# Decode attention on one core: keys transposed inside their load buffers, queries and results moved in single transfers

## The chip, the core and the metric

The kernel runs on one core of a Trainium2 chip. The core has a matrix engine (TensorE, "PE" in the profile; its weight loads are listed as "PEld"), a vector engine (VectorE, "DVE"), a scalar engine (ScalarE, "ACT"), GpSimd ("POOL") and SyncE ("SP"), which here only issues transfers. Sixteen DMA engines move data between the chip's main memory (HBM) and the on-chip memory SBUF; matmul results go to a smaller memory, PSUM. Both on-chip memories have 128 partitions. The metric is the device time of one execution in microseconds (us), and a kernel's time is the median of several runs.

## The reference

One query token attends to 65,536 cached tokens, with 32 query heads and 8 key/value heads, in bfloat16. Four query heads share a key/value head.

```python
B, Hq, Hkv, Sq, Sk, D = 1, 32, 8, 1, 65536, 128
k = jnp.repeat(k, Hq // Hkv, axis=1)
v = jnp.repeat(v, Hq // Hkv, axis=1)
scores = jnp.einsum("bhqd,bhkd->bhqk", q, k) * D ** -0.5
p = jax.nn.softmax(scores, axis=-1)
return jnp.einsum("bhqk,bhkd->bhqd", p, v)
```

Keys and values are 134.2 MB each. Every byte of them is read once and used by four query heads.

## The kernel before

**Loads.** A key/value head's keys are loaded in four steps of 128 partitions x 128 tokens x 128 numbers, 4 MB each (`k_load`, L118 to L122); values likewise (`v_load`, L196). All of these loads are issued by SP, in program order, into four rotating buffers of 32 KB per partition (`iopool`, L56): a load can be issued only when the work on the load four places ahead of it, in the same buffer, has let that buffer go. The order of loads is: four key steps of head 0; then for each head g from 1 to 7 a key step of head g and a value step of head g-1 in turn; at the end four value steps of head 7, the last of which is cut into six pieces.

**Scores.** `k_step(g, s, kn)` (L124) computes the scores of one key step. DVE transposes the keys in 32 x 32 blocks, taking two bfloat16 numbers as one 4-byte element; each transposition (L135) takes two of the eight groups w = 0..7 into a separate tile `T` (three buffers, `tpool`, L57). PE then runs four matmuls for each group (L144), 32 per key step, accumulated in one PSUM bank `sc` (three buffers, L62). ACT copies the finished bank into `S_g` (L151). The weights of these matmuls, `wq`, hold the four queries of the head at a shifted place in a tile of zeros; `queries(g)` (L104) fills them from `qx`, the transposed queries.

**Queries.** At the start ACT's queue issues four transfers of the 32 query rows (256 bytes each) into the four quarters of the partitions of `qn` (L69, L70). DVE transposes `qn` to `qx` (L100) and copies the first head's queries to `wq` (L109) before it starts on the keys.

**Softmax and values.** When a head's four steps of scores are in, `softmax(g)` finds the maximum, ACT takes the exponential over all scores with row sums (L177), and DVE transposes the result to `ET` (L190). `v_stream` (L202 to L213) multiplies each value step with `ET`, 32 matmuls per step, accumulated in `psum_o`; `pick` (L224, L230) reduces that to the head's 128 numbers per query.

**Results.** `finish(g0, n)` sums the partial results of n heads with one matmul, takes the reciprocal of the sums of exponentials (`sums`, L237, L239), and `store` scales (L244) and stores them (L250): heads 0 to 3 at once while head 4's values are next, heads 4 to 6 at once near the end. `finish_last` handles head 7, whose last value step is worked off token by token as its pieces land.

Engines run their own instructions in order. A scheduler places the instructions of all parts on each engine; within the part at stake, PE has the 32 score matmuls of a key step and then the 32 matmuls of the value step that was loaded after it.

Of the kernel before, what the change touches and what calls it, by code (L numbers as in the profile page):

```python
# [8 lines left out]
ALU = mybir.AluOpType  # L9
# [5 lines left out]
NW = 16  # L15
# [5 lines left out]
def kernel(  # L21
# [17 lines left out]
    nc = tc.nc  # L39
    P = nc.NUM_PARTITIONS  # L40
    B, Hq, Sq, D = q.shape
    _, Hkv, Sk, _ = k.shape
    assert B == 1 and Sq == 1 and D == P
    HPG = Hq // Hkv
# [7 lines left out]
    fp32 = mybir.dt.float32  # L52
    bf16 = mybir.dt.bfloat16

    const = ctx.enter_context(tc.tile_pool(name="const", bufs=1))
    iopool = ctx.enter_context(tc.tile_pool(name="iopool", bufs=4))  # L56
    tpool = ctx.enter_context(tc.tile_pool(name="tpool", bufs=3))  # L57
    spool = ctx.enter_context(tc.tile_pool(name="spool", bufs=2))
    epool = ctx.enter_context(tc.tile_pool(name="epool", bufs=2))
    opool = ctx.enter_context(tc.tile_pool(name="opool", bufs=2))  # L60
    stats = ctx.enter_context(tc.tile_pool(name="stats", bufs=2))
    psc = ctx.enter_context(tc.tile_pool(name="psc", bufs=3, space=bass.MemoryType.PSUM))  # L62
    psm = ctx.enter_context(tc.tile_pool(name="psm", bufs=1, space=bass.MemoryType.PSUM))
    psf = ctx.enter_context(tc.tile_pool(name="psf", bufs=1, space=bass.MemoryType.PSUM))
    pso = ctx.enter_context(tc.tile_pool(name="pso", bufs=2, space=bass.MemoryType.PSUM))


    qn = const.tile([P, D], bf16)
    for a in range(4):  # L69
        nc.scalar.dma_start(out=qn[32 * a:32 * a + 32, :], in_=q[0, :, 0, :])  # L70


    WX = P + 32
# [1 line left out]
    for x in range(2):  # L75
# [8 lines left out]
        out=sel[:, :], in_=ident[:, :].rearrange("p (x h) -> p h x", h=HPG), axis=AX.X, op=ALU.max  # L84
# [3 lines left out]
        out=blk[:, :], in_=ident[:, :].rearrange("p (j w h) -> p w j h", w=W, h=HPG), axis=AX.XY, op=ALU.max  # L88
# [6 lines left out]
    nc.gpsimd.memset(one[:, :], 1.0)  # L95
    lsum_all = const.tile([P, Hkv], fp32)
    o_all = const.tile([P, Hkv, D], fp32)

    qx = const.tile([P, D], bf16)
    nc.vector.transpose(out=qx[:, :].bitcast(fp32), in_=qn[:, :].bitcast(fp32))  # L100
# [3 lines left out]
    def queries(g):  # L104
        eng = nc.vector if g == 0 else nc.gpsimd
        wv = Wq[g % 2][:, :].rearrange("p (b r x) -> p b r x", b=2, r=2)
        for a in range(4):
            qd = slice(32 * a, 32 * a + 32)
            eng.tensor_copy(  # L109
                out=wv[qd, :, :, 32 * a + 28:32 * a + 28 + HPG],  # L110
                in_=qv[qd, :, :, g * HPG:(g + 1) * HPG],
            )

    queries(0)

    S_tiles, E_tiles, ET_tiles, o_tiles = {}, {}, {}, {}

    def k_load(g, s):  # L118
        kn = iopool.tile([P, NT, D], bf16, name="kn", tag="io", align_bytes=2048)
        src = k[0, g].rearrange("(p n) d -> p n d", p=P)  # L120
        nc.sync.dma_start(out=kn[:, :, :], in_=src[:, s * NT:(s + 1) * NT, :])
        return kn  # L122

    def k_step(g, s, kn):  # L124
        if s == 0:
            S_tiles[g] = spool.tile([P, KT, 4 * P], fp32, name="S_g")
        wq = Wq[g % 2]
        kv = kn[:, :, :].rearrange("p (c w) d -> p w c d", w=W)
        sc = psc.tile([P, 4 * P], fp32, name="sc")
        for w in range(W):  # L130
            if s == 0 and w == W // 2 and g > 0:
                transpose_weights(g - 1)
            if w % 2 == 0:
                T = tpool.tile([P, 2, NW, D], bf16, name="T")
                nc.vector.transpose(  # L135
                    out=T[:, :, :, :].bitcast(fp32),
                    in_=kv[:, w:w + 2].bitcast(fp32),
                )
            Tv = T[:, w % 2].rearrange("p n (b i r) -> p n b i r", b=2, r=2)
            for b in range(2):  # L140
                for r in range(2):
                    bp = 2 * b + r
                    at = bp * WX + 28 - 4 * w
                    nc.tensor.matmul(  # L144
                        out=sc[:, :],
                        lhsT=wq[:, at:at + P],
                        rhs=Tv[:, :, b, :, r],
                        start=(w == 0 and bp == 0),
                        stop=(w == W - 1 and bp == 3),
                    )  # L150
        nc.scalar.copy(out=S_tiles[g][:, s, :], in_=sc[:, :])  # L151

    def softmax(g):
        S_g = S_tiles[g]
# [32 lines left out]
    def transpose_weights(g):  # L187

        ET = epool.tile([P, KT, NW, 32], bf16, name="ET")
        nc.vector.transpose(  # L190
            out=ET[:, :, :, :].rearrange("p s c x -> p (s c x)"),
            in_=E_tiles[g][:, :, :].rearrange("p s x -> p (s x)"),
        )
        ET_tiles[g] = ET

    def v_load(g, s, pieces=(NT,)):  # L196
        vb = iopool.tile([P, NT, D], bf16, name="vb", tag="io", align_bytes=2048)
        src = v[0, g].rearrange("(p n) d -> p n d", p=P)
        x = 0
        for step in pieces:  # L200
            n0 = s * NT + x
            nc.sync.dma_start(out=vb[:, x:x + step, :], in_=src[:, n0:n0 + step, :])  # L202
            x += step
        return vb

    def v_stream(g, s, vb, rows, last):

        if s == 0:
            o_tiles[g] = pso.tile([P, 4, D], fp32, name="psum_o")
        for c in range(rows // W):  # L210
            for x in range(2):
                j = 2 * x + c % 2
                nc.tensor.matmul(  # L213
                    out=o_tiles[g][32 * j:32 * j + 32, :, :],
                    lhsT=ET_tiles[g][:, s, c, :],
                    rhs=vb[:, c * W + 4 * x:c * W + 4 * x + 4, :],
                    start=(s == 0 and c < 2),
                    stop=(last and c >= rows // W - 2),
                )

    def pick(g):

        o_m = opool.tile([P, 4, D], fp32, name="o_m")
        nc.vector.tensor_tensor(  # L224
            out=o_m[:, :, :],
            in0=o_tiles[g][:, :, :],
            in1=mask[:, :].unsqueeze(2).broadcast_to([P, 4, D]),
            op=ALU.mult,
        )
        nc.vector.tensor_reduce(  # L230
            out=o_all[:, g, :], in_=o_m[:, :, :].rearrange("p x d -> p d x"), axis=AX.X, op=ALU.add
        )

    def sums(g0, n):

        psum_l = psm.tile([HPG, n], fp32, name="psum_l", tag="misc")
        nc.tensor.matmul(out=psum_l[:, :], lhsT=sel[:, :], rhs=lsum_all[:, g0:g0 + n], start=True, stop=True)  # L237
        rl = stats.tile([HPG, n], fp32, name="rl")
        nc.vector.reciprocal(out=rl[:, :], in_=psum_l[:, :])  # L239
        return rl  # L240

    def store(g0, n, psum_f, rl):
        o_out = stats.tile([HPG, n, D], bf16, name="o_out")
        nc.vector.tensor_tensor(  # L244
            out=o_out[:, :, :],
            in0=psum_f[:, :, :],
            in1=rl[:, :].unsqueeze(2).broadcast_to([HPG, n, D]),
            op=ALU.mult,
        )
        nc.scalar.dma_start(  # L250
            out=out[0, :, 0, :].rearrange("(g h) d -> h g d", h=HPG)[:, g0:g0 + n, :], in_=o_out[:, :, :]
        )

    def finish(g0, n):
        rl = sums(g0, n)
        psum_f = psf.tile([HPG, n, D], fp32, name="psum_f", tag="fin")
        nc.tensor.matmul(  # L257
            out=psum_f[:, :, :], lhsT=sel[:, :], rhs=o_all[:, g0:g0 + n, :], start=True, stop=True
        )
        store(g0, n, psum_f, rl)  # L260

    def finish_last(g, s, vb):

# [43 lines left out]
    for g in range(Hkv + 1):  # L307
        if 0 < g < Hkv:
            queries(g)
        for s in range(KT):  # L310
            if g < Hkv:
                k_step(g, s, k_load(g, s))
            elif s == 0:
                transpose_weights(g - 1)
            if g > 0:
                last = s == KT - 1
                if g == Hkv and last:
                    finish_last(g - 1, s, v_load(g - 1, s, pieces=(64, 32, 16, 8, 4, 4)))
                else:
                    v_stream(g - 1, s, v_load(g - 1, s), NT, last)  # L320
                    if last:
                        pick(g - 1)
                    if last and g % 4 == 0:
                        finish(g - 4, 4)
                    if last and g == Hkv - 1:
                        finish(g - g % 4, g % 4)
        if g < Hkv:
            softmax(g)

# [29 lines left out]
```

## Time and profile before

| | |
|---|---|
| Median of 3 runs | 631.85 us (631.57 to 631.90) |
| Profiled execution, its time | 631.69 us |
| Profiled execution, its span (first to last instruction) | 629.6 us |
| PE busy | 363.2 us (58%) |
| DVE busy | 340.4 us (54%) |
| ACT busy | 36.8 us (6%) |
| POOL busy | 6.4 us (1%) |
| HBM read | 268.47 MB, 426 GB/s over the span |
| Mean granted clock of TensorE | 0.780 |

The page also cuts the span into 40 equal slices of 15.74 us and gives, for each, the busy share of each engine in tenths, the granted clock of PE, the mean busy share of the 16 DMA engines and the data rate. A group line names the line of the kernel, the engine, the operation, the tile written and the tiles read with their shapes, then the count, the total busy time in us and the mean of one in ns, and after a second bar the idle time of that engine before these instructions and what ended most of it. In a timeline, the first two columns are the start and the length in us, and an entry may merge several instructions of one line ("x16"). A DMA queue line gives packets, megabytes and the share of the time of the 16 DMA engines.

### The profile page before, as it was taken

Reading aid. Unit: us, or ns where it says so; the run is one execution under the profiler, and the core shown is the slowest. Engines: PE = TensorE matmul, PEld = TensorE weight load, DVE = VectorE, ACT = ScalarE, POOL = GpSimd, SP = SyncE. Lnnn points to the kernel's source line nnn. Section 1 sums busy time; section 2 is a strip of 40 time slices with the busy share of each in tenths; the row PEclk is TensorE's granted clock in tenths of the full one; section 3 lists DMA queues with packets and bytes.
Section 4 is the critical chain, followed back from the end, with each engine's and each line's share of the span. In section 5 each row is a group of like instructions: output and inputs, shape, how many; then the busy total and the mean of one; then the engine's idle time right before and its main releaser. Section 6 shows DMA issues by size and latency. Waiting matters only on the chain.

```text
span 629.6 us, 4872 instructions
## 1 busy us (share of the span) xinstructions
PE 363.2 (58%) x2133; PEld 141.5 (22%) x2133; DVE 340.4 (54%) x201; ACT 36.8 (6%) x49; POOL 6.4 (1%) x37
## 2 busy tenths in 40 slices
PE   0686836745557554575645856447665466644645
PEld 0232312211222221222211222112221122211212
DVE  0998833774337753377543775436754366553511
ACT  0000100010000100001000010001000010000100
POOL 0000000000000000000000000000000000000000
PEclk9998988767887677876778867788677787767856
DMA  8999999999999999999999999999999999999996
GB/s 369 433 434 431 433 432 434 432 433 433 432 433 432 433 433 432 433 432 433 432 433 433 430 434 434 433 432 433 435 432 433 432 433 433 432 433 434 431 430 267
DMA packets 10192, 268.78 MB, mean 427 GB/s; under 512 B 1340, under 2 KB 1596, under 8 KB 1852
## 3 DMA queue, kind: packets, MB, share of 16 engines
q1 hardware_dynamic: 9936, 268.44, 99.0%
q8 instruction: 16, 0.26, 0.1%
q10 hardware_dynamic: 236, 0.04, 0.0%
q14 instruction: 4, 0.03, 0.0%
HBM read 268.47 MB, written 0.01 MB: 426 GB/s over the span
## 4 chain that ended last, share of the span: by engine, by line
DMA 73%; DVE 12%; issue 11%; PE 2%; ACTq 0%; DVEq 0%; SPq 0%
DMA kn<-in_k_dram 66%; DVE T L135 12%; DMA vb<-in_v_dram 5%; DMA qn<-in_q_dram 2%; PE sc L144 2%; PE psum_o L213 0%; PE psum_oT L290 0%; ACTq L70 0%; PE psum_f L280 0%; DVEq L135 0%; DVE wq L109 0%; PE psum_f L287 0%; DVE sel L83 0%; DVE o_last L302 0%; SPq L202 0%
## 5 line engine op out<-in xcount | busy, mean ns | idle before, releaser
L144 PE MATMUL sc<-T,wq 128*128 128x512 bf16 x1024 | 287.9, 445 | 220.2 <-DVE T L135 220.2
L135 DVE STREAM_TRANSPOSE T<-kn 128x2048 f32<-128x2048 f32 x128 | 284.2, 2277 | 198.6 <-DMA kn<-in_k_dram 198.6
L144 PEld LDWEIGHTS <-wq 128*128 128x128 bf16 x1024 | 109.5, 109 | 394.6 <-issue 159.5
L213 PE MATMUL psum_o<-vb,ET 128*32 128x512 bf16 x1008 | 65.1, 403 | 12.0 <-DMA vb<-in_v_dram 9.8
L151 ACT COPY S_g<-sc 128x512 f32<-128x512 f32 x32 | 18.8, 587 | 510.8 <-PE sc L144 510.8
L213 PEld LDWEIGHTS <-ET 128*32 128x32 bf16 x1008 | 25.5, 100 | 49.2 <-issue 28.3
L156 DVE TENSOR_REDUCE mx<-S_g 128x1 f32<-128x2048 f32 x8 | 18.3, 2286 | 26.1 <-ACT S_g L151 26.1
L190 DVE STREAM_TRANSPOSE ET<-E_g 128x2048 bf16<-128x2048 bf16 x8 | 18.5, 2311 | 16.3 <-ACT E_g L177 16.3
L177 ACT ACTIVATE E_g<-S_g,nmb 128x2048 bf16<-128x2048 f32 x8 | 16.0, 2001 | 47.6 <-DVE nmb L174 40.4
L224 DVE TENSOR_TENSOR o_m<-psum_o,mask 128x512 f32<-128x512 f32 x8 | 5.5, 682 | 21.5 <-PE psum_o L213 21.5
L109 POOL COPY wq<-qx 32x16 bf16<-32x16 bf16 x28 | 5.3, 190 | 426.9 <-PE sc L144 410.2
L160 PE MATMUL psum_t<-ident,mx 128*1 128x128 f32 x8 | 2.2, 270 | 11.2 <-DVE mx L156 11.2
L100 DVE STREAM_TRANSPOSE qx<-qn 128x64 f32<-128x64 f32 x1 | 0.2, 245 | 15.0 <-DMA qn<-in_q_dram 15.0
L172 PE MATMUL psum_b<-one,mrow 1*128 1x1 f32 x16 | 3.5, 288 | 8.3 <-DVE mrow L166 8.3
L230 DVE TENSOR_REDUCE o_all<-o_m 128x128 f32<-128x512 f32 x8 | 8.0, 1000 | 0.0
L172 PEld LDWEIGHTS psum_b<-one,mrow 1*128 1x128 f32 x16 | 3.0, 232 | 12.2 <-issue 11.4
L237 PE MATMUL psum_l<-lsum_all,sel 128*4 128x4 f32 (+2 forms) x6 | 0.6, 166 | 7.7 <-ACT E_g L177 7.7
L257 PE MATMUL psum_f<-o_all,sel 128*4 128x512 f32 (+1 forms) x4 | 2.6, 730 | 2.9 <-DVE o_all L230 2.9
L160 PEld LDWEIGHTS psum_t<-ident,mx 128*1 128x1 f32 x8 | 0.6, 79 | 15.1 <-DVE mx L156 11.6
L174 DVE COPY nmb<-psum_b 128x1 f32<-128x1 f32 x8 | 1.2, 152 | 2.9 <-PE psum_b L172 2.9
L290 PE MATMUL psum_oT<-ET,vb 128*128 128x4 bf16 x56 | 1.8, 167 | 1.4 <-DMA vb<-in_v_dram 1.4
L244 DVE TENSOR_TENSOR o_out<-psum_f,rl 4x512 bf16<-4x512 f32 (+1 forms) x2 | 1.2, 612 | 2.5 <-PE psum_f L257 2.5
(30 smaller groups left out, 16.1 us busy)
## 6 DMA issues: line engine op xcount, KB each, us to landing
kn<-in_k_dram SPq DMA_DIRECT2D x32, 4096.0 KB, 29.6
vb<-in_v_dram SPq DMA_DIRECT2D x31, 4096.0 KB, 34.1
vb<-in_v_dram SPq DMA_DIRECT2D x1, 2048.0 KB, 29.5
vb<-in_v_dram SPq DMA_DIRECT2D x1, 1024.0 KB, 31.6
vb<-in_v_dram SPq DMA_DIRECT2D x1, 512.0 KB, 32.3
vb<-in_v_dram SPq DMA_DIRECT2D x1, 256.0 KB, 32.5
vb<-in_v_dram SPq DMA_DIRECT2D x2, 128.0 KB
qn<-in_q_dram ACTq DMA_DIRECT2D x4, 8.0 KB, 10.1
```

Of the source, the lines that this page charges most:

```text
L109: eng.tensor_copy(out=wv[qd, :, :, 32 * a + 28:32 * a + 28 + HPG], in_=qv[qd, :, :, g * HPG:(g + 1) * HPG],)
L135: nc.vector.transpose(out=T[:, :, :, :].bitcast(fp32), in_=kv[:, w:w + 2].bitcast(fp32),)
L144: nc.tensor.matmul(out=sc[:, :], lhsT=wq[:, at:at + P], rhs=Tv[:, :, b, :, r], start=(w == 0 and bp == 0), stop=(w == W - 1 and bp == 3),)
L151: nc.scalar.copy(out=S_tiles[g][:, s, :], in_=sc[:, :])
L156: nc.vector.tensor_reduce(out=mx[:, :], in_=S_g[:, :, :].rearrange("p n c -> p (n c)"), axis=AX.X, op=ALU.max)
L160: nc.tensor.transpose(out=psum_t[:, :], in_=mx[:, :], identity=ident[:, :])
L172: nc.tensor.matmul(out=psum_b[:, :], lhsT=mrow[:, :], rhs=one[:, :], start=True, stop=True)
L177: nc.scalar.activation(out=E_g[:, :, :].rearrange("p s x -> p (s x)"), in_=S_g[:, :, :].rearrange("p s x -> p (s x)"), func=ACT.Exp, bias= ...
L190: nc.vector.transpose(out=ET[:, :, :, :].rearrange("p s c x -> p (s c x)"), in_=E_tiles[g][:, :, :].rearrange("p s x -> p (s x)"),)
L213: nc.tensor.matmul(out=o_tiles[g][32 * j:32 * j + 32, :, :], lhsT=ET_tiles[g][:, s, c, :], rhs=vb[:, c * W + 4 * x:c * W + 4 * x + 4, :], ...
L224: nc.vector.tensor_tensor(out=o_m[:, :, :], in0=o_tiles[g][:, :, :], in1=mask[:, :].unsqueeze(2).broadcast_to([P, 4, D]), op=ALU.mult,)
L230: nc.vector.tensor_reduce(out=o_all[:, g, :], in_=o_m[:, :, :].rearrange("p x d -> p d x"), axis=AX.X, op=ALU.add)
```

## The change

Five edits:

1. The separate tile `T` is gone. DVE transposes four of the eight groups at a time, and writes the result back over the keys in the load buffer. The score matmuls read the load buffer itself.
2. The score banks are allocated in pairs (two buffers of two banks in place of three of one), and ACT copies a pair at once, after the second and the fourth key step of a head.
3. The 32 query rows go to the four quarters of the partitions in one transfer, whose source repeats the rows four times (a leading dimension of 4 with a step of 0).
4. The results of heads 0 to 6 collect in one tile and are stored in one transfer, after head 6 is finished.
5. `finish` runs for two heads at a time (heads 0 and 1, 2 and 3, 4 and 5), and once for head 6 alone.

```diff
-    tpool = ctx.enter_context(tc.tile_pool(name="tpool", bufs=3))
...
-    psc = ctx.enter_context(tc.tile_pool(name="psc", bufs=3, space=bass.MemoryType.PSUM))
+    psc = ctx.enter_context(tc.tile_pool(name="psc", bufs=2, space=bass.MemoryType.PSUM))
...
-    for a in range(4):
-        nc.scalar.dma_start(out=qn[32 * a:32 * a + 32, :], in_=q[0, :, 0, :])
+    nc.scalar.dma_start(out=qn[:, :], in_=q[0, :, 0, :].unsqueeze(0).broadcast_to([4, Hq, D]))
...
+    o_out = const.tile([HPG, Hkv - 1, D], bf16)
...
-        sc = psc.tile([P, 4 * P], fp32, name="sc")
+        if s % 2 == 0:
+            sc_tiles[g] = psc.tile([P, 2, 4 * P], fp32, name="sc")
+        sc = sc_tiles[g][:, s % 2, :]
...
-            if w % 2 == 0:
-                T = tpool.tile([P, 2, NW, D], bf16, name="T")
-                nc.vector.transpose(
-                    out=T[:, :, :, :].bitcast(fp32),
-                    in_=kv[:, w:w + 2].bitcast(fp32),
-                )
-            Tv = T[:, w % 2].rearrange("p n (b i r) -> p n b i r", b=2, r=2)
+            if w % 4 == 0:
+                groups = kv[:, w:w + 4].bitcast(fp32)
+                nc.vector.transpose(out=groups, in_=groups)
+            Tv = kv[:, w].rearrange("p n (b i r) -> p n b i r", b=2, r=2)
...
-        nc.scalar.copy(out=S_tiles[g][:, s, :], in_=sc[:, :])
+        if s % 2 == 1:
+            nc.scalar.copy(out=S_tiles[g][:, s - 1:s + 1, :], in_=sc_tiles[g][:, :, :])
...
-    def store(g0, n, psum_f, rl):
-        o_out = stats.tile([HPG, n, D], bf16, name="o_out")
...
-        nc.scalar.dma_start(
-            out=out[0, :, 0, :].rearrange("(g h) d -> h g d", h=HPG)[:, g0:g0 + n, :], in_=o_out[:, :, :]
-        )
...
-        store(g0, n, psum_f, rl)
+        nc.vector.tensor_tensor(
+            out=o_out[:, g0:g0 + n, :],
+            in0=psum_f[:, :, :],
+            in1=rl[:, :].unsqueeze(2).broadcast_to([HPG, n, D]),
+            op=ALU.mult,
+        )
...
-                    if last and g % 4 == 0:
-                        finish(g - 4, 4)
+                    if last and g % 2 == 0:
+                        finish(g - 2, 2)
                     if last and g == Hkv - 1:
-                        finish(g - g % 4, g % 4)
+                        finish(g - 1, 1)
+                        nc.scalar.dma_start(
+                            out=out[0, 0:g * HPG, 0, :].rearrange("(g h) d -> h g d", h=HPG), in_=o_out[:, :, :]
+                        )
```

More of the change, by code (lines that the diff above doesn't have):

```diff
@@ L114 @@
     queries(0)
-    S_tiles, E_tiles, ET_tiles, o_tiles = {}, {}, {}, {}
+    S_tiles, sc_tiles, E_tiles, ET_tiles, o_tiles = {}, {}, {}, {}, {}
     def k_load(g, s):
@@ L144, in k_step @@
                     nc.tensor.matmul(
-                        out=sc[:, :],
+                        out=sc,
                         lhsT=wq[:, at:at + P],
@@ L240, in sums @@
         return rl
-    def store(g0, n, psum_f, rl):
-        o_out = stats.tile([HPG, n, D], bf16, name="o_out")
[L244 to L248, printed above, removed]
-        )
-        nc.scalar.dma_start(
-            out=out[0, :, 0, :].rearrange("(g h) d -> h g d", h=HPG)[:, g0:g0 + n, :], in_=o_out[:, :, :]
-        )
     def finish(g0, n):
```

## The prediction

> **What bounds the kernel now.** I read the page from the top: busy shares, the slices, the DMA queues, the costliest groups.
>
> ```profile
> GB/s 369 433 434 431 433 432 434 432 433 433 432 433 432 433 433 432 433 432 433 432 433 433 430 434 434 433 432 433 435 432 433 432 433 433 432 433 434 431 430 267
> ...
> q1 hardware_dynamic: 9936, 268.44, 99.0%
> ...
> q10 hardware_dynamic: 236, 0.04, 0.0%
> ...
> L144 PE MATMUL sc<-T,wq 128*128 128x512 bf16 x1024 | 287.9, 445 | 220.2 <-DVE T L135 220.2
> L135 DVE STREAM_TRANSPOSE T<-kn 128x2048 f32<-128x2048 f32 x128 | 284.2, 2277 | 198.6 <-DMA kn<-in_k_dram 198.6
> ```
>
> The loads' queue (q1) fills 99.0% of 16 engines, and the rate stands at 433 GB/s in every slice but the first and the last. DVE waits for keys 198.6 us, PE for DVE 220.2 us. So the DMA engines set the time: a 4 MB load (4.194 MB) takes 4.194 / 433 = 9.69 us, and a change costs or saves what it does to the stream's start, its end, or to gaps in it. Next come the places where a gap could open: the start, in the timelines of DVE and SP, then of PE.
>
> ```profile
> 16.57 0.24 DVE L100 STREAM_TRANSPOSE qx<-qn 128x64 f32<-128x64 f32 x1 [15.03 <-DMA qn<-in_q_dram]
> ...
> 18.11 35.20 DVE L135 STREAM_TRANSPOSE T<-kn 128x2048 f32<-128x2048 f32 x16
> ```
>
> ```profile
> 0.74 26.61 SPq L121 DMA_DIRECT2D kn<-in_k_dram  x5
> 35.80 0.33 SPq L202 DMA_DIRECT2D vb<-in_v_dram  x1
> 44.57 0.33 SPq L121 DMA_DIRECT2D kn<-in_k_dram  x1
> ```
>
> ```profile
> 20.47 12.87 PE L144 MATMUL sc<-T,wq 128*128 128x512 bf16 x48 [20.47 <-DVE T L135]
> 33.63 1.90 PE L144 MATMUL sc<-T,wq 128*128 128x512 bf16 x8 [0.29 <-DVE T L135]
> ```
>
> DVE stands idle for the queries until 16.57 and starts on keys at 18.11. Four loads are issued at once from 0.74; the fifth needs the first buffer back and goes out at the end of the merged entry, near 27. The fourth load lands near 41.5 (the longest issue-to-landing time of a key load is 39.7 us, for a load issued near 1.8). So the fifth has 41.5 - 27 = 14.5 us in hand. That reserve is the number to keep in mind.
>
> Last, what the small transfers do, by DMA views of the first 30 us and of the stretch 355 to 378 us.
>
> ```profile
> q10 hardware_dynamic: 192, 0.03, 0.6%
> ...
> qn<-in_q_dram ACTq DMA_DIRECT2D x4, 8.0 KB, 10.1
> ```
>
> ```profile
> q10 hardware_dynamic: 20, 0.00, 0.1%
> ...
> out_dram<-o_out ACTq DMA_DIRECT2D x1, 4.0 KB
> ```
>
> Each transfer has, besides its rows, one completion packet on each engine that it uses. Four query transfers of 32 rows: 192 packets = 4 x (32 + 16), so 16 engines, 2 rows and a completion on each. The store of four heads, whose leading dimension is 4 on both sides: 20 = 16 rows + 4, so four engines with four rows each. And rows share the engines with the key stream: by their issue-to-landing times (5.9, median 10.1, 14.3 us; issues at 0.74 to 2.12) the first query transfer landed at 0.74 + 5.9 = 6.65, the last at 2.12 + 14.33 = 16.45. That is 9.80 us for the last three transfers' nine packets per engine, 1.09 us per 256-byte packet. A key row of 32 KB on one engine takes 32,768 / (433 / 16 GB/s) = 1.21 us, and a load gives each engine eight such rows and one short completion: 8 x 1.21 / 9 = 1.08 us per entry. So each small packet waits for one entry of the key queue.
>
> **The change part by part.** *Queries in one transfer: +15.2 us.* The source now leads with a dimension of 4, the destination with 128 partitions. No transfer in the trace has sides that differ, so bounds: if the 128 partitions decide, as for the key loads and the old query transfers, 16 engines take eight rows and a completion each; if the 4 decides, as in the store, four engines take 32 rows and a completion each, 33 packets. I take four: the store is the one row with a leading 4, and a transfer has to be cut alike on both sides. The 33rd packet then comes 30 packets after the third, at 6.65 + 30 x 1.09 = 39.35. (Upper bound, every packet behind a full key row: 6.65 + 30 x 1.21 = 42.95.) From there, on DVE, whose order still puts queries before keys:
>
> - queries' landing to first key transposition: 18.11 - 16.45 = 1.66, so 41.0;
> - two transpositions of four groups. Elsewhere four of the old ones in a row take 8.89 us, so 4.44 each: done at 45.45 and 49.9. In place and spread over the buffer, one could differ from the dense form; nearest rows are 4 x 2.256 and 4 x 2.312 (fastest and slowest of the 128), 9.02 and 9.25 us as singles, so +0.4 us at most;
> - PE's 16 matmuls of the first half. The first 48 took 12.87 us: weight loads beside them are spaced 0.427 us for the first 11, the other 37 in 7.93, 0.214 each. So 11 x 0.427 + 5 x 0.214 = 5.8, until 51.25; the second half 16 x 0.214 = 3.4, until 54.65. Bounds: all fast, 49.9 + 3.4 = 53.3; all slow, 45.45 + 32 x 0.427 = 59.1. That covers slower reading of keys that now lie 2 KB apart;
> - the buffer comes free only now, since the matmuls read it. SP issues the fifth load at 54.7. The stream was empty from 41.5. An issue into an empty queue costs 41.5 - 0.74 - 4 x 9.69 = 2.0 us beyond the transfer itself, so the load lands at 54.7 + 2.0 + 9.69 = 66.4, where it landed at 41.5 + 9.69 = 51.2: 15.2 us later.
>
> What is late next: key steps 2 to 4 come free one transposition time apart, at 62.3, 71.2 and 80.1 (DVE 8.89 per step, then 3.4 of PE), and the loads ahead of theirs end at 66.4, 76.1 and 85.8: 2.0 us of lead suffice in each. The ninth load needs head 1's first key step, held up by the maximum of head 0: transposed in halves until 81 and 88 with the maximum (copy 1.05, reduction 2.29) between, matmuls until 92 to 95; the eighth load ends at 95.5, so 0 to 1.5 us more; I take 0. Then keys come only every 19.4 us and DVE catches up.
>
> The Trainium skill has a rule against this edit ("DMA: Bandwidth & Descriptors", section "Rules for kernel authors"): a leading broadcast of c copies in the source confines the whole transfer to at most c engines. By it the term is the 15.2 us above; by the old query transfers' row, 16 engines, it would be nothing. The 20-packet store agrees for a leading 4; no row here shows a broadcast.
>
> *Keys in place: 0 in the steady state.* 128 transpositions become 64 with the same elements. Release moves from DVE's end to PE's. For the step at 461.13 DVE was done at 470.02 and PE at 473.2 (32 matmuls in 9.73 from 463.50); with halves PE starts at 465.6 and ends at about 475.3, so the buffer is 5.3 us later. Three loads (29.1 us) lie between this one's landing and the need for its successor: at 461.1 + 29.1 - 2.0 = 488.2. Cover: 12.9 us; behind SP's wait stands the next value load, whose buffer is free at 477. At a head's end the softmax is some 2.5 us later (2.1 of PE, 0.5 of the wider copy), the next key step starts that much later: still under the cover. If it were gone, each of 28 such releases would cost up to 5.3 us.
>
> *Copies in pairs, stores, sums: 0.* The pair copy is between 0.59 and 1.17 us against 0.59, on ACT, which is busy 6%. For head 7 the softmax chain ends at 600.4 and the first two value steps take PE 3.6 us each; +2.6 leaves PE done at 610.2, before the third lands at 616.0. One store of 28 rows has eight packets on each of four engines, 8 x 1.09 = 9 us from about 598, with nobody waiting before the end at 627. Two sums and two scalings more, under 1 us of DVE each, fall where DVE waits for keys (10 us per step).
>
> Sum: 631.69 + 15.2 = 646.9, said as **647.0 us**. The profiled execution lies 0.16 us below the median of the runs, which is nothing here.
>
> **Rivals.** *A, the forecast.* Speaks for it: 20 packets. Its own range: packets all fast and PE all fast, 643.9 (15.2 - 1.35 - 1.6 for an issue that needs 0.4); PE all slow, +4.5, and the upper landing of the queries, +3.6: 655.
>
> *B, not slower: the queries use 16 engines.* Nine packets per engine: the third at 6.65, six more at 1.09, 13.2. DVE would start keys at 14.9, 3.2 us before now; the first buffer is free by 14.9 + 8.9 + 3.4 + 2.4 = 29.6, 11.9 before 41.5. No gap, nothing won, as the stream was full already: 631.7. The edge lies where the queries land at 41.5 - 2.0 - 15.3 = 24.2; below that, no loss. Against it: the store's packets.
>
> *C, matmuls on the spread keys run at the slow 0.427 throughout*, on top of A. A key step then takes 13.7 us of PE, over the 9.69 of a load: the first buffer comes at 59.1 (+4.5), and the next three 13.7 apart, 4.0 us each: 647 + 4.5 + 12 = 663. In the steady state 13.7 + 1.9 stays below 19.4. Against it: the old matmuls too read every second number.
>
> *D, faster*: fewer instructions shorten something I don't see. 630.
>
> **How the numbers follow.** A 0.82, B 0.12, C 0.04, D 0.02. The range 643 to 655 holds A; with B, C and D outside it leaves out 0.18. A measurement of this kernel tells a change over 0.2% (1.26 us): slower A and C, 0.86; same B, 0.12; faster D, 0.02.
>
> **What would show it.** Right: DVE's first query transposition near 39 and the first key one near 41; 132 packets in the small queue at the start (128 + 4); the DMA row with a hole of 13 to 17 us after 41.5 in slices 3 and 4, then 433 GB/s to the end; the fifth load issued by PE's release near 55. Wrong: queries at 13 with 144 packets (B); PE at over 0.4 us per matmul past its first dozen (C); holes at the heads' changes.

## The result and the profile after

The changed kernel takes 649.61 us (median, 649.33 to 649.78) against 631.88 us: 1.0281 times as long, with a 95% interval of 1.0264 to 1.0297. That is 17.7 us more; the forecast was 15.2 us more. The profiled execution took 649.33 us with a span of 647.5 us.

First the page of the changed kernel: data rate in 40 slices, now of 16.19 us each, the two queues, and the two costliest groups.

```profile
GB/s 389 420 229 162 428 443 422 439 434 421 436 437 421 447 425 432 441 423 434 437 424 443 426 430 442 425 431 438 427 434 435 428 441 427 434 435 426 435 432 265
...
q1 hardware_dynamic: 9936, 268.44, 96.4%
...
q10 hardware_dynamic: 172, 0.04, 0.0%
...
L142 PE MATMUL sc<-kn,wq 128*128 128x512 bf16 x1024 | 280.3, 437 | 239.0 <-DVE kn L136 228.9
L136 DVE STREAM_TRANSPOSE kn<-kn 128x4096 f32<-128x4096 f32 x64 | 280.0, 4417 | 177.2 <-DMA kn<-in_k_dram 177.2
```

The rate row has one hole, in the third and fourth slice. Against 433 GB/s it is worth (433 - 229) / 433 x 16.19 + (433 - 162) / 433 x 16.19 = 7.6 + 10.1 = 17.7 us, the whole loss. All later slices lie around the old rate. The transpositions and the score matmuls keep DVE and PE busy for slightly less than before (280.0 against 284.2 us, 280.3 against 287.9), and it buys nothing.

Next the start of the changed kernel, in the timelines of DVE, of PE with its weight loads, and of SP (start and length in us).

```profile
42.88 0.24 DVE L99 STREAM_TRANSPOSE qx<-qn 128x64 f32<-128x64 f32 x1 [41.34 <-DMA qn<-in_q_dram]
...
44.42 39.05 DVE L136 STREAM_TRANSPOSE kn<-kn 128x4096 f32<-128x4096 f32 x9
```

```profile
48.91 12.29 PE L142 MATMUL sc<-kn,wq 128*128 128x512 bf16 x48 [48.91 <-DVE kn L136]
...
51.83 5.32 PEld L142 LDWEIGHTS <-wq 128*128 128x128 bf16 x25 [0.25 <-issue]
...
61.89 3.64 PE L142 MATMUL sc<-kn,wq 128*128 128x512 bf16 x16 [0.68 <-DVE kn L136]
```

```profile
0.74 57.04 SPq L120 DMA_DIRECT2D kn<-in_k_dram  x5
65.56 0.33 SPq L201 DMA_DIRECT2D vb<-in_v_dram  x1
...
94.70 0.33 SPq L120 DMA_DIRECT2D kn<-in_k_dram  x1
```

The queries are in at 42.88 where they were in at 16.57. Keys are begun at 44.42, and SP's merged entry of five key loads ends at 57.78, so the fifth load was issued at 57.45, some 15 us after the four loads before it had been delivered. In the DMA view of the first 50 us, the small queue has 132 packets, and nothing moves after the four key loads:

```profile
GB/s 0 367 288 419 472 499 420 473 420 421 420 420 420 420 420 420 420 421 420 420 420 420 420 420 420 395 446 420 420 420 420 420 420 0 0 0 0 0 0 0
...
q10 hardware_dynamic: 132, 0.03, 0.3%
```

132 = 128 rows + 4 completions: four engines. Before, it was 192 = 128 + 64. The fifth load, issued with the queue empty, took 12.0 us to land, by the DMA view of 40 to 60 us:

```profile
kn<-in_k_dram SPq DMA_DIRECT2D x1, 4096.0 KB, 12.0
```

### The profile page after: what moved, and what is told of

It is laid out like the page before. It is cut to its first block, busy times and chain, and to the rows that moved or that the text cites. A ratio compares the mean times of both kernels' runs of the same rounds, so it can differ in the third digit from the quotient of the medians.

```text
span 647.5 us, 4722 instructions
## 1 busy us (share of the span) xinstructions
PE 356.6 (55%) x2141; PEld 141.8 (22%) x2141; DVE 337.1 (52%) x141; ACT 34.3 (5%) x33; POOL 6.5 (1%) x37
## 4 chain that ended last, share of the span: by engine, by line
DMA 60%; PE 21%; DVE 17%; ACT 0%; issue 0%; DVEq 0%; ACTq 0%
DMA kn<-in_k_dram 50%; PE sc L142 20%; DVE kn L136 16%; DMA qn<-in_q_dram 7%; DMA vb<-in_v_dram 4%; PE psum_o L212 1%; DVE ET L189 0%; DVE mx L155 0%; ACT E_g L176 0%; DVE o_all L229 0%; PE psum_f L272 0%; ACT S_g L150 0%; PE psum_oT L282 0%; DVE wq L108 0%; DVE o_m L223 0%
## 5 line engine op out<-in xcount | busy, mean ns | idle before, releaser
L142 PE MATMUL sc<-kn,wq 128*128 128x512 bf16 x1024 | 280.3, 437 | 239.0 <-DVE kn L136 228.9
L136 DVE STREAM_TRANSPOSE kn<-kn 128x4096 f32<-128x4096 f32 x64 | 280.0, 4417 | 177.2 <-DMA kn<-in_k_dram 177.2
L150 ACT COPY S_g<-sc 128x1024 f32<-128x1024 f32 x16 | 16.2, 1014 | 535.5 <-PE sc L142 535.5
L244 PE MATMUL psum_f<-o_all,sel 128*4 128x256 f32 (+1 forms) x8 | 3.1, 484 | 5.7 <-DVE o_all L229 5.7
L247 DVE TENSOR_TENSOR o_out<-psum_f,rl 4x256 bf16<-4x256 f32 (+1 forms) x4 | 1.5, 379 | 3.0 <-PE psum_f L244 3.0
```

Of the source, the lines that this page charges most:

```text
L136: nc.vector.transpose(out=groups, in_=groups)
L142: nc.tensor.matmul(out=sc, lhsT=wq[:, at:at + P], rhs=Tv[:, :, b, :, r], start=(w == 0 and bp == 0), stop=(w == W - 1 and bp == 3),)
L150: nc.scalar.copy(out=S_tiles[g][:, s - 1:s + 1, :], in_=sc_tiles[g][:, :, :])
L244: nc.tensor.matmul(out=psum_f[:, :, :], lhsT=sel[:, :], rhs=o_all[:, g0:g0 + n, :], start=True, stop=True)
```

## The experiments

Each kernel ran beside the kernel before on the same chip. Medians of the kernel before were 632.06 us beside the first four and 631.89 us beside the last three.

### The queries in four transfers again, all other edits kept

```diff
-    nc.scalar.dma_start(out=qn[:, :], in_=q[0, :, 0, :].unsqueeze(0).broadcast_to([4, Hq, D]))
+    for a in range(4):
+        nc.scalar.dma_start(out=qn[32 * a:32 * a + 32, :], in_=q[0, :, 0, :])
```

> The changed kernel with the queries in four transfers again, all other edits kept. Theory (the whole loss is the queries' landing, and nothing else in the change reaches the load stream): queries land near 16.5, first key transposition near 18.1, the fifth load goes out near 31.7 (18.1 + 13.6) with ten us in hand before 41.5, no hole in the stream; 631.7 us, within 0.6 of before. Rival (the later release of the key buffers, or the wider copies and sums, cost something of their own): 634 or more, with holes at the heads' changes.

Measured: 632.21 us, ratio 1.0007 (0.9996 to 1.0018): no difference from the kernel before. Its DVE and SP timelines:

```profile
16.80 0.24 DVE L100 STREAM_TRANSPOSE qx<-qn 128x64 f32<-128x64 f32 x1 [15.25 <-DMA qn<-in_q_dram]
...
18.34 34.72 DVE L137 STREAM_TRANSPOSE kn<-kn 128x4096 f32<-128x4096 f32 x8
53.44 4.45 DVE L137 STREAM_TRANSPOSE kn<-kn 128x4096 f32<-128x4096 f32 x1 [0.38 <-DMA kn<-in_k_dram]
```

```profile
0.74 31.73 SPq L121 DMA_DIRECT2D kn<-in_k_dram  x5
39.48 0.33 SPq L202 DMA_DIRECT2D vb<-in_v_dram  x1
```

The fifth load goes out at 32.1, more than nine us before the four loads ahead of it end near 41.5, and the stream has no hole: every slice of its rate row from the second to the 38th lies between 430 and 437 GB/s. So with the queries on time, keys in place, paired copies, one store and sums by two cost nothing that can be measured. The steady state is as worked out before: for a key step that DVE began at 461.23 (it had waited for the keys), the buffer's next load went out at 475.45, 14.2 us later; in the kernel before it was 470.05 for a step begun at 461.13, 8.9 us later. The 5.3 us are real and hidden. The four lines, first of the kernel before, then of this run:

```profile
461.13 8.89 DVE L135 STREAM_TRANSPOSE T<-kn 128x2048 f32<-128x2048 f32 x4 [8.70 <-DMA kn<-in_k_dram]
470.05 0.33 SPq L121 DMA_DIRECT2D kn<-in_k_dram  x1
```

```profile
461.23 8.77 DVE L137 STREAM_TRANSPOSE kn<-kn 128x4096 f32<-128x4096 f32 x2 [6.23 <-DMA kn<-in_k_dram]
475.45 0.33 SPq L121 DMA_DIRECT2D kn<-in_k_dram  x1
```

### The kernel before with the queries in one transfer, no other edit

```diff
-    for a in range(4):
-        nc.scalar.dma_start(out=qn[32 * a:32 * a + 32, :], in_=q[0, :, 0, :])
+    nc.scalar.dma_start(out=qn[:, :], in_=q[0, :, 0, :].unsqueeze(0).broadcast_to([4, Hq, D]))
```

> The kernel before with the queries in one transfer, and no other edit. Theory: the queries land near 42.9 as in the changed kernel; but the first key buffer is free when DVE has read it, 8.9 us after the first transposition starts at 44.4, not after PE's last matmul at 57.5; so the fifth load goes out at 53.4, 4 us earlier, and the time is 649.6 - 4.1 = 645.5 (644.5 to 646.5). Rival (the queries' landing explains all of the 17.7 us by itself): 649.6. Rival (in-place keys carry most of it): under 640.

Measured: 647.54 us, ratio 1.0247 (1.0233 to 1.0261): 15.5 us lost by the query transfer alone, and 2.1 us less than the changed kernel, not 4.1, outside the 644.5 to 646.5 expected. The SP timeline and the rate row (slices of 16.12 us) show why:

```profile
0.74 52.76 SPq L120 DMA_DIRECT2D kn<-in_k_dram  x5
...
79.49 0.33 SPq L201 DMA_DIRECT2D vb<-in_v_dram  x1
93.67 0.33 SPq L120 DMA_DIRECT2D kn<-in_k_dram  x1
```

```profile
GB/s 389 422 232 266 438 399 424 423 442 435 422 435 443 422 425 448 427 425 446 429 424 445 431 424 436 439 424 433 437 430 429 440 431 425 440 435 422 439 435 264
```

The fifth load is issued at 53.17, 4.3 us before the changed kernel's, as expected, and the hole in the third and fourth slice is worth 13.7 us in place of 17.7. But the sixth slice stands at 399: (433 - 399) / 433 x 16.12 = 1.3 us are lost a second time. That is the ninth load, issued at 93.67, which needs the buffer of head 1's first key step. In this kernel DVE does that step in four quarters with the pieces of head 0's softmax between them, and all loads before it end 4 us earlier than in the changed kernel; the reserve is used up. In the changed kernel the ninth load goes out at 94.70 with the stream 4 us behind, and there is no second hole. So the expectation's 4.1 us for the earlier release were right at that release, and 1.3 of them were given back at the ninth load. The spans agree with that difference: 644.7 to 645.6 us here and 647.5 to 648.0 for the changed kernel, 2.8 apart in the middle. The times differ by less, 2.1, because these executions took 1.7 to 3.5 us beyond their spans and the changed kernel's 1.8 to 1.9; the reason stays open.

### The one query transfer ahead of the key loads, in SP's queue

```diff
-    nc.scalar.dma_start(out=qn[:, :], in_=q[0, :, 0, :].unsqueeze(0).broadcast_to([4, Hq, D]))
+    nc.sync.dma_start(out=qn[:, :], in_=q[0, :, 0, :].unsqueeze(0).broadcast_to([4, Hq, D]))
```

> The changed kernel with the one query transfer issued by SP, ahead of the key loads, in their queue. Theory (each small packet waits for a key packet of the same engine, and four engines are slow only for that): with no key packets ahead the 33 packets of an engine take a few us at most, queries land before 6, the key stream starts 1 to 3 us later for the longer issue and the packets ahead of it; 632.5 to 635. Rival (a transfer with a leading broadcast of 4 is slow by itself): queries land later than 20, over 636.

Measured: 632.17 us, ratio 1.0003 (0.9994 to 1.0012). The queries now stand in the loads' queue. In the DMA view of the first 3.1 us it has 146 packets, 14 key rows and again 132 small ones, so the engines are four as in the changed kernel:

```profile
q1 hardware_dynamic: 146, 0.49, 56.7%
```

```profile
3.09 0.24 DVE L99 STREAM_TRANSPOSE qx<-qn 128x64 f32<-128x64 f32 x1 [1.55 <-DMA qn<-in_q_dram]
```

The queries are in at 3.1 us in place of 42.9. Four engines are no handicap for 32 KB; standing behind key packets is. The expected cost of 1 to 3 us for a later start of the keys did not come: SP issued the first key load at 1.51 in place of 0.74, and the median is within 0.2 us of before. So one query transfer can be kept at no cost, and at no gain over the kernel before.

### The one query transfer with the 32 rows as its leading dimension

```diff
-in_=q[0, :, 0, :].unsqueeze(0).broadcast_to([4, Hq, D])
+in_=q[0, :, 0, :].unsqueeze(1).broadcast_to([Hq, 4, D])
```

> The changed kernel with one query transfer whose source leads with the 32 rows and repeats each four times (step 0 in the second dimension). Partition 4h+a then holds query h, so the heads are in the wrong places and the output is not the reference's; the work and its order are unchanged. Theory (the leading dimension of the source sets the number of engines): 16 engines, 8 rows and a completion each, 144 packets, landing near 15; 631.7 us. Rival (one transfer in place of four, or a repeated source, is what makes it late): 132 packets or a landing near 43, 649.6.

Measured: 631.45 us, ratio 0.9992 (0.9983 to 1.0001). The DMA view of its first 60 us:

```profile
q10 hardware_dynamic: 144, 0.03, 0.3%
...
qn<-in_q_dram ACTq DMA_DIRECT2D x1, 32.0 KB, 14.7
```

144 = 128 + 16: sixteen engines, and a landing at 0.74 + 14.7 = 15.4. One transfer, a source that repeats each row four times with step 0, the same bytes, the same queue, and no loss. So the order of the source's dimensions decides, and neither the number of transfers nor the repetition.

### The queries in two transfers with a leading dimension of 2

```diff
-    nc.scalar.dma_start(out=qn[:, :], in_=q[0, :, 0, :].unsqueeze(0).broadcast_to([4, Hq, D]))
+    for a in range(2):
+        nc.scalar.dma_start(out=qn[64 * a:64 * a + 64, :], in_=q[0, :, 0, :].unsqueeze(0).broadcast_to([2, Hq, D]))
```

> The changed kernel with the queries in two transfers, each of which fills 64 partitions from a source that leads with a dimension of 2. Theory (leading dimension sets the engines, and a small packet waits for one entry of the key queue only while there is one): two engines take 64 rows and 2 completions each, 132 packets in all; half of them are still queued when the key stream runs dry near 42.7, and the rest then goes at once; landing 43 to 45, time 649.5 to 652. Rival (a small packet costs some 1.1 us whatever else runs): landing near 6 + 66 x 1.1 = 78, some 684 us.

Measured: 650.15 us, ratio 1.0287 (1.0270 to 1.0304).

```profile
43.00 0.24 DVE L100 STREAM_TRANSPOSE qx<-qn 128x64 f32<-128x64 f32 x1 [41.46 <-DMA qn<-in_q_dram]
```

The small queue again has 132 packets, now 128 + 2 x 2. Each of two engines carries 66 small packets, twice as many as in the changed kernel, and yet the queries land at the same time within 0.2 us. A small packet waits for one key packet only as long as there are key packets; when the four loads are through, the rest goes in a moment. In the DMA view of 42 to 43 us of this run, 65 of the 132 go within that one us:

```profile
q10 hardware_dynamic: 65, 0.02, 7.1%
q1 hardware_dynamic: 1, 0.00, 0.1%
```

So with two engines the landing is set by the end of the four loads issued ahead, not by the count of packets. With four engines the two fall together: in the changed kernel the last 8 of the 132 go between 40 and 43 us, beside the last 32 packets of the key loads, so no run tells there which of the two sets the landing.

### Three load buffers, in the kernel before and with keys in place

```diff
-    iopool = ctx.enter_context(tc.tile_pool(name="iopool", bufs=4))
+    iopool = ctx.enter_context(tc.tile_pool(name="iopool", bufs=3))
```

The second of the two also has the queries in four transfers.

> The kernel before with three load buffers in place of four. A load must then go out within 2 x 9.69 - 2.0 = 17.4 us of the landing of the load three places ahead. Key buffers are held 9.4 us after landing, 11 to 12.3 at a head's change, 14.6 and 15.2 near the start: no hole, 631.7 us (up to 633). If reserves below 4 us already cost: over 634.

> The changed kernel with four query transfers and three load buffers. Key buffers are held 13.4 to 15.0 us after landing, and 17.4 to 19.8 at a head's change, where 17.4 is allowed: holes of 0 to 2.4 us at seven changes of head, some 8 us in all, and 2 to 4 at the start; 637 to 646 us. Theory (the cover of 9 us or more that four buffers leave is all that hides the later release). Rival (release is not what the stream waits for): 631.7, as with three buffers in the kernel before.

Measured: 632.85 us (1.0015, 1.0006 to 1.0025) for the kernel before with three buffers (its profiled execution, the shortest of ten at 631.85, has no hole), and 650.75 us (1.0302, 1.0285 to 1.0320) for keys in place with three. The rate row of the latter (slices of 16.25 us):

```profile
GB/s 389 387 386 448 419 422 446 424 431 348 427 444 419 448 330 431 440 418 452 358 452 419 438 428 330 444 426 433 435 390 431 438 423 448 344 437 418 450 421 263
```

Holes stand at the start (387, 386) and then at the last six of the seven changes of head (348, 330, 358, 330, 344, a smaller one at 390). With one buffer less, keys in place and the edits that come with them (the paired copies among them) cost 18.9 us, and the kernel before 1.0: it was the cover of the fourth buffer that made the later release free. The size was 5 us over the range. At the change of head near 153 us, SP's timeline and the DMA view of 145 to 160 us have the price of one hole:

```profile
152.91 0.33 SPq L202 DMA_DIRECT2D vb<-in_v_dram  x1
```

```profile
vb<-in_v_dram SPq DMA_DIRECT2D x1, 4096.0 KB, 13.5
```

This load was issued when the queue had just run dry and took 13.5 us to land, 3.8 beyond the 9.69 of its transfer; the expectation had counted 2.0. What makes up the difference was not tried.

## Why the prediction was right, by its steps

- **Bound by the stream, changed only by its gaps: right.** The whole loss stands in two slices, and the rest of the kernel is unchanged in rate.
- **The leading dimension of 4 decides, on four engines: right**, shown by 132 packets against 144 when only the order of the source's dimensions is turned. The rule of the Trainium skill that the prediction weighed ("DMA: Bandwidth & Descriptors", section "Rules for kernel authors": a leading broadcast of c copies keeps a transfer on at most c engines) is confirmed here for 4 and for 2; rival B is out.
- **Landing of the queries at 39.35: mis-sized.** It was 42.85. The spacing was nearly right: 132 packets on four engines end at 42.85, and from the landing of the transfer that leads with 32 rows (nine packets per engine, 15.4) there are 24 packets more in 27.4 us, 1.14 each against the 1.09 taken. What failed was the starting point. I let the single transfer start where the first of the four had started; but nine packets landing at 15.4 put its first packet near 15.4 - 8 x 1.09 = 6.7, while twelve landing at 16.45 put the old one near 16.45 - 11 x 1.09 = 4.5. These two account for 2.2 + 24 x 0.05 = 3.4 of the 3.5 us. The DMA views agree that it started later: the small queue has 16 packets in the first 4 us of the kernel before, and one in the first 6 us of the changed kernel. The upper bound of 42.95 held it. What the prediction did not have is that small packets wait only while key packets last; here the 33 packets of an engine ran out at about the same moment, so the sum hardly felt it.
- **From landing to the fifth load's issue, 15.3 us: measured 14.6.** 1.57 to the first key transposition (1.66 said), and 13.03 from there to the issue (13.65 said). DVE's part was as said: PE began 4.49 after the first transposition did (4.44 said). PE's 32 matmuls took 8.5 us, not 9.2: by the weight loads beside them seven matmuls were spaced 0.42 us and the other 25 took 5.32, where the prediction had counted eleven slow ones as in the kernel before. Why there were fewer, no run shows. Reading keys 2 KB apart did not slow PE: 16 matmuls at full pace take 3.64 us, where 8 took 1.90 before. Rival C is out.
- **An issue into an empty queue costs 2.0 us: measured 2.3** (12.0 us from issue to landing in the DMA view of 40 to 60 us, less 9.69).
- **Sum.** 3.5 - 0.7 + 0.3 = 3.1 us more than said; the whole was 2.5 more. The place from which the loss was counted was off too: the fifth load was put at 51.2 without a hole, and by the DMA views of the kernel before its last packet went between 52.2 and 52.4. In the changed kernel that packet went between 69.0 and 69.2, 16.8 us later. The other 0.9 of the 17.7 us are not placed by these views and stay open. So the mechanism was right and the sizes were off in both directions: that the figure came within 2.6 us owes something to luck.
- **The second stage, "0 to 1.5 us, I take 0": right in the changed kernel**, and shown to be a near miss: in the kernel before with the late queries the same load opens a second hole of 1.3 us.
- **Keys in place hidden by 12.9 us of cover, the rest at nothing: right**, by the ratio 1.0007 without the query edit, and by the 18.9 us (1.0 in the kernel before) when a buffer is taken away.

## What to carry to other kernels

A small transfer that runs beside a saturated stream is priced by the number of its packets on the busiest engine, each at about the time of one stream packet (here 1.1 us), until the packets issued ahead of it are through; so look at the leading dimension of its source, and issue it ahead of the stream rather than beside it when anything waits for it. A saving on an engine that waits for the stream is worth nothing, and an edit that holds a load buffer longer is worth nothing either way only while the reserve lasts: write down both numbers, the hold and the allowance, for the steady state and for the start. When two edits share a reserve, their costs do not add: the earlier release gave 4.3 us at one load and lost 1.3 of them four loads later.

## What the runs showed of the hardware

- A transfer of 128 rows on four engines landed 2.3 us after its issue with no key packets ahead of it, and 42.1 us after its issue beside four key loads: the same transfer, 18 times as long.
- The first packet of a single transfer of 128 rows came some 2.2 us later beside the key loads than that of a transfer of 32 rows. Its issue was 1.15 us long on ACT's queue with the source leading with 4, and 0.59 us with the source leading with 32, so the length of the issue is not the reason; the reason stays open.
- A load issued as the queue runs dry lost 2.3 us at the start, where all engines were idle, and 3.8 us in mid-stream with three buffers.
